# A decode layer on one core: the last 96 rows of w2 on 32 partitions, c and x in one transfer, the first load whole, and another order of TensorE's last work

## The chip, the core and the metric

The kernel runs on one core of a Trainium2 chip. The metric is the device time of one execution in microseconds; the median of several executions counts. A profiled execution lists the work of the engines (TensorE is PE, its weight loads PEld; VectorE is DVE, ScalarE is ACT, GpSimd is POOL, SyncE is SP), the DMA queues, and which event ended each wait.

## The reference

A layer with adaptive layer norm: attention of one new token over a cache, then a dense block with Mish. Two batches, D = 512, 32 heads of 128, 4096 cached keys a head, F = 1376, all float32.

```python
mod = (_silu(c) @ w_mod).reshape(c.shape[0], 6, 1, -1)
sa, ca, ga, sb, cb, gb = (mod[:, 0], mod[:, 1], mod[:, 2], mod[:, 3], mod[:, 4], mod[:, 5])
h = _layernorm(x, axis=-1) * (1 + ca) + sa
x = x + ga * _A_ref(h, A_k_cache, A_v_cache, A_wq, A_wo)
h = _layernorm(x, axis=-1) * (1 + cb) + sb
x = x + gb * _B_ref(h, B_w1, B_b1, B_w2)
```

`_A_ref` projects q with `wq`, takes softmax(q k / sqrt(128)) v for each head and projects with `wo`. `_B_ref` is `mish(h @ w1 + b1) @ w2`.

## The kernel before

**Loads.** All large inputs (297 MB, nearly all of it the caches) are laid out on the host as rows of 128 partitions and go through three rooms of 128 x 16384 floats (8 MB each, 64 KB a partition). `stream()` (L30) lists 36 loads. Load 0 is m01 (the two modulations of the first norm), wq 0 and wq 1 in one transfer of 4 MB, and k 0 in another of 4 MB. Loads 1 to 31 are one transfer of 8 MB each: the keys of a head, values that lie further back, now and then a piece of wq and wo. The last four hold the remaining values and weights in smaller transfers; load 35 has m3 and w1 in two, m5 and w2 in four (L62). `load(n)` (L133) issues a room's transfers on SP; `used(...)` (L145) issues load n + 3 when everything of load n has been used. So three rooms are asked for at the start, and the fourth when head 0's keys have been used. ACT issues three small transfers: c and x (L162, 8 rows each, on every 16th partition) and `bias` (L164, one row of 12 floats on each of 128 partitions).

**Start.** PE runs in program order: c's columns (`cps`), the two means of the first norm, then `fps`, a PSUM tile that starts with b1 for all hidden units (L269, from `bias`) and gets `h @ w1` much later; then modulation 0 (L271), the columns of the normed x, and q for eight heads (L294).

**Heads.** For each head VectorE multiplies the keys with q in place (`products`, L321) and sums over 128 (`sums`, L324); the end of the sums gives the room back. PE does the weighted sums of the values (`weighted_v`, L362) and the output projection, a few heads behind.

**Tail.** The last head, 31, is treated by itself. Its values come in two halves of `weighted_v` into bank `ov0`; between the halves stand four `fold` matmuls, which bring the output projection of the other heads into `xps` (L474), and modulation 4 (L478). After the halves come `value_sums`, `head_values` and `head_out_q` (L484), then the residual x2, the second norm (`centred`, `rstd`), modulation 3, `h2ps`, the product with w1 (L514), three matmuls that add it to `fps` (L529), modulation 5, the Mish on VectorE and ScalarE up to `actt` (L549), and the product with w2 into `yps` (L554). `busy(n)` (L297) issues matmuls whose result nobody reads.

The 1376 hidden units are 11 chunks of up to 128, each on partitions of its own; chunk 10 has 96 units, and its other 32 rows of w2 are zeros. `yps` takes the chunks in order, 4 matmuls of 128 columns a chunk, one for each group of 32 output partitions; an fp32 matmul is two instructions here. Then VectorE multiplies with modulation 5 and adds x2 (L562, L563), and SP writes the output. w2 lies in load 35 behind m5: chunks 0 to 4 come with m5, chunks 5 to 8 in a transfer of 1 MB, chunks 9 and 10 in 256 KB each.

Of the kernel before, what the change touches and what calls it, by code (L numbers as in the profile page):

```python
# [8 lines left out]
F32 = mybir.dt.float32  # L9
# [4 lines left out]
P = 128  # L14
# [8 lines left out]
    "k": BIG, "v": HALF, "wq": W, "wo": W, "m01": 2 * W, "m2": W, "m3": W, "m4": W, "m5": W,  # L23
    "w1": 4 * sum(WIDTHS), "w2": 512 * len(CHUNKS),
}
AHEAD = (14, 22)
ROW = 2 * BIG


def stream():  # L30


    order, n_v = [], 0
    for h in range(1, HEADS):
# [12 lines left out]
    loads = [[([("m01", 0), ("wq", 0), ("wq", 1)], (4 * W,)), ([("k", 0)], (BIG,))]]  # L47
    for _ in range(1, HEADS):
        row = []
        while size(row) < ROW:  # L50
            room = ROW - size(row)
            row += order.pop(next(i for i, x in enumerate(order) if size(x) <= room))
        loads.append([(row, (ROW,))])
    last = [("v", h, i) for h in range(HEADS - 4, HEADS) for i in range(2)]
    assert order == [[key] for key in last[:2]], order
    loads += [
        [(last[:2] + [("wo", 6), ("wo", 7), ("m2", 0)], (BIG + 3 * W,))],
        [(last[2:4], (BIG,)), (last[4:6], (BIG,))],
        [([("m4", 0)] + last[6:], (W + HALF, W, W))],
        [  # L60
            ([("m3", 0), ("w1", 0)], (W + 2 * sum(WIDTHS), 2 * sum(WIDTHS))),
            ([("m5", 0), ("w2", 0)], (W + 5 * 512, 4 * 512, 512, 512)),  # L62
        ],
    ]
    return loads
# [3 lines left out]
def kernel(  # L69
# [28 lines left out]
    SCALE = DH ** -0.5  # L98
    NCH = len(CHUNKS)

    const = ctx.enter_context(tc.tile_pool(name="const", bufs=1))
# [13 lines left out]
    def take(t, keys):  # L115
        lo = 0
        for key in keys:
            kind, n = key[:2]
            part = t[:, lo : lo + SIZES[kind]]
            lo += SIZES[kind]  # L120
            if kind == "k":
                k_t[n] = part.rearrange("p (j d) -> p j d", d=DH)
            elif kind == "v":
                v_t[n, key[2]] = part.rearrange("p (c n) -> p c n", n=512)
            elif kind in ("wq", "wo"):
                (wq_t if kind == "wq" else wo_t)[n] = part.rearrange("p (k n) -> p k n", k=G)
            else:
                w_t[kind] = part.rearrange("p (k n) -> p k n", k=NCH if kind == "w2" else G)

# [3 lines left out]
    def load(n):  # L133

        t = kvp.tile([P, ROW], F32, tag="room", name=f"room{n}", bufs=3)
        lo = 0
        for keys, srcs in loads[n]:
            take(t[:, lo:], keys)
            for src in srcs:
                nc.sync.dma_start(out=t[:, lo : lo + src.shape[-1]], in_=src)  # L140
                lo += src.shape[-1]
# [15 lines left out]

    cq = work.tile([P, P], F32, tag="xn", name="cq", bufs=1)
    xq = const.tile([P, P], F32, name="xq")
    for t, src in ((cq, head[0]), (xq, head[1])):  # L160
        nc.gpsimd.memset(t, 0.0)
        nc.scalar.dma_start(out=t[::TB, :], in_=src)  # L162
    bias = const.tile([P, NCH + 1], F32, name="bias")
    nc.scalar.dma_start(out=bias, in_=b1c)  # L164
# [28 lines left out]
    h2t = const.tile([P, G, R], F32, name="h2t")  # L193
    actt = const.tile([P, NCH, R], F32, name="actt")
    for t in (ct, h2t, actt):
# [71 lines left out]

    fps = psum.tile([P, 512], F32, tag="att2", name="fps", bufs=1)[:, : NJ * G * B]
    nc.tensor.matmul(fps, lhsT=ident, rhs=bias[:, :, None].to_broadcast([P, NJ * G, B]), start=True, stop=False, skip_group_check=True)  # L269

# [200 lines left out]
    xps = psum.tile([P, 512], F32, tag="att", name="xps", bufs=1)  # L471
    weighted_v(H - 1, 0, 1 - N % 2)
    for g in range(G):
# [54 lines left out]
    for j in range(NJ):  # L528
# [4 lines left out]
            start=False,  # L533
            stop=(j == NJ - 1),
            skip_group_check=True,
        )
    busy(6)
    gps = modulation("5", 1, wm5)
    f = const.tile([P, 3, NJ * G, B], F32, name="f")
    hid = fps.rearrange("p (n b) -> p n b", b=B)  # L540
# [7 lines left out]
    nc.vector.reciprocal(f[:, 2], f[:, 2])  # L548
    nc.vector.tensor_tensor(out=actt[:, :, ::TB], in0=f[:, 1, :NCH], in1=f[:, 2, :NCH], op=ALU.mult)  # L549

    yps = wide_ps("yps")
    for n in range(NCH):
        for t in range(G):
            nc.tensor.matmul(  # L554
                yps[R * t : R * (t + 1), :P],
                lhsT=actt[:, n, :],
                rhs=w2_t[:, n, P * t : P * (t + 1)],
                start=(n == 0),
                stop=(n == NCH - 1),
            )  # L560
# [6 lines left out]
def _lay_out(np, a):  # L567
# [19 lines left out]
    starts = np.cumsum((0,) + WIDTHS)  # L587
    b1c = np.zeros((P, 12), a["B_b1"].dtype)
    w2 = np.zeros((P, len(CHUNKS), 512), a["B_w2"].dtype)
    for n, (g, j) in enumerate(CHUNKS):  # L590
        f0 = starts[g] + P * j
        f1 = min(f0 + P, starts[g + 1])
        b1c[: f1 - f0, n] = a["B_b1"][f0:f1]
        w2[: f1 - f0, n] = a["B_w2"][f0:f1]

# [3 lines left out]
    def piece(kind, n, part=None):  # L599
# [3 lines left out]
    arrays = {  # L603
        "head": np.stack([q_rows(a["c"]), q_rows(a["A_x"])]),
        "b1c": b1c,
    }
    for n, parts in enumerate(stream()):
        for i, (keys, widths) in enumerate(parts):
            row = np.concatenate([piece(*key) for key in keys], axis=1)
            cuts = np.split(row, np.cumsum(widths)[:-1], axis=1)  # L610
            for j, t in enumerate(cuts):
                arrays[f"load{n}_{i}_{j}"] = np.ascontiguousarray(t)
    return arrays
# [24 lines left out]
```

## Time and profile before

| | |
|---|---|
| median of three runs | 698.67 us (698.63 to 698.77) |
| the profiled execution | 698.77 us |
| its span, first to last instruction | 696.9 us |
| mean granted clock of TensorE | 0.677 |
| DMA, mean over the span | 427 GB/s |
| VectorE, PE, ScalarE busy | 587.1, 284.6, 44.3 us |

A page gives busy time by engine, the span in 40 slices (each digit tenths of a slice), the DMA queues (packets, megabytes, share of 16 engines' time) and the chain of waits that ended last. In the chain in order of time each row is start, length and what the chain passed through. A timeline row has start, length, engine, line, operation, tiles written and read, shapes, count, and in brackets the idle time before it and what ended it. A row of stretches has the length and then, for each engine, busy time and count of instructions, at the end the granted clock, the share of DMA time and GB/s. A row of DMA issues has count, KB each and the time from issue to landing.

### The profile page before, as it was taken

To read this page: it belongs to the slowest core of one execution; us is meant where nothing else is said; L and a number is where in the kernel's file an instruction comes from. 1 tells how busy PE (TensorE), PEld (TensorE's weight loads), DVE (VectorE), ACT (ScalarE), POOL (GpSimd) and SP (SyncE) were. 2 spreads that over 40 slices of the span, in tenths; PEclk is the share of its full clock that TensorE was granted. 3 is DMA by queue.
4 is the path that set the end of the run, shared out by engine and by line. 5 is a ranking of instruction groups with operands and counts; after the bars stand their busy time and mean duration, and the time that the engine had idled before them with its cause. 6 is when DMAs were issued, how large, how long until landed. Compare 5 with 4: busy or idle time off the path is not lost.

```text
span 696.9 us, 3922 instructions
## 1 busy us (share of the span) xinstructions
PE 284.6 (41%) x1640; PEld 103.9 (15%) x1640; DVE 587.1 (84%) x219; ACT 44.3 (6%) x169; POOL 4.2 (1%) x20
## 2 busy tenths in 40 slices
PE   0603334335145615234342806234333425224697
PEld 0200011001011201101110301011101111001245
DVE  3399999999999999999999999999999999899002
ACT  1000000000000000000000000000000000000011
POOL 2000000000000000000000000000000000000000
PEclk9966656768565567656575656656575658556889
DMA  9999999999999999999999999999999999999996
GB/s 388 455 421 421 425 467 429 418 430 425 463 422 421 437 421 456 429 421 441 421 451 429 418 444 425 448 426 421 441 429 445 429 421 441 429 434 422 425 419 266
DMA packets 6690, 297.48 MB, mean 427 GB/s; under 512 B 888, under 2 KB 912, under 8 KB 1168
## 3 DMA queue, kind: packets, MB, share of 16 engines
q1 hardware_dynamic: 6496, 297.21, 98.9%
q8 instruction: 13, 0.21, 0.1%
q10 hardware_dynamic: 176, 0.01, 0.0%
q14 instruction: 5, 0.04, 0.0%
HBM read 297.22 MB, written 0.00 MB: 426 GB/s over the span
## 4 chain that ended last, share of the span: by engine, by line
DMA 63%; DVE 33%; PE 2%; issue 0%; SPq 0%; POOL 0%; ACT 0%; ACTq 0%; DVEq 0%; POOLq 0%
DMA room<-in_load 61%; DVE room L321 16%; DVE s L324 16%; DMA bias<-in_b1c 3%; PE ov L362 1%; PE qps L294 1%; PE modps L247 1%; PE yps L554 0%; SPq L140 0%; DVE m L337 0%; DVE hcw L283 0%; DVE m L329 0%; PE fps L269 0%; ACT q L295 0%; ACTq L162 0%
## 5 line engine op out<-in xcount | busy, mean ns | idle before, releaser
L321 DVE TENSOR_TENSOR room<-room,q 128x8192 f32<-128x8192 f32 x32 | 278.1, 8691 | 40.0 <-DMA room<-in_load 35.5
L324 DVE TENSOR_REDUCE s<-room 128x64 f32<-128x8192 f32 x32 | 277.9, 8683 | 0.0
L362 PE MATMUL ov<-room,e 128*32 128x512 f32 x1024 | 177.0, 841 | 73.5 <-ACT e L340 31.2
L333 PE MATMUL mt<-d,same 128*128 128x64 f32 x64 | 18.7, 388 | 194.0 <-DVE d L331 194.0
L362 PEld LDWEIGHTS ov<-room,e 128*32 128x32 f32 x1024 | 39.8, 146 | 180.8 <-issue 128.3
L340 ACT ACTIVATE e<-s,m 64x64 f32<-64x64 f32 x64 | 22.1, 345 | 547.9 <-DVE m L337 547.1
L333 PEld LDWEIGHTS mt<-d,same 128*128 128x128 f32 x64 | 13.5, 263 | 224.6 <-DVE d L331 177.6
L294 PE MATMUL qps<-room,hcw 128*128 128x512 f32 x64 | 40.7, 797 | 4.6 <-DMA room<-in_load 3.8
L348 PE MATMUL l<-l,ones 128*128 128x8 f32 x16 | 4.6, 359 | 73.7 <-ACT e L340 73.7
L385 PE MATMUL otp<-pick,o 128*128 128x8 f32 (+2 forms) x72 | 14.4, 328 | 37.3 <-ACT o L377 35.4
L377 DVE COPY o<-ov 128x256 f32<-128x256 f32 x1 | 0.4, 423 | 25.1 <-ACT o L377 25.1
L385 PEld LDWEIGHTS otp<-pick,o 128*128 128x128 f32 x72 | 13.6, 282 | 46.6 <-ACT o L377 43.7
L294 PEld LDWEIGHTS qps<-room,hcw 128*128 128x128 f32 x64 | 15.9, 261 | 24.4 <-issue 18.6
L348 PEld LDWEIGHTS l<-l,ones 128*128 128x128 f32 x16 | 3.8, 296 | 75.1 <-ACT e L340 75.1
L393 PE MATMUL att<-room,ot 128*32 128x512 f32 x62 | 10.9, 756 | 5.2 <-DMA room<-in_load 4.7
L337 DVE TENSOR_REDUCE m<-mt 128x1 f32<-128x64 f32 x32 | 6.9, 217 | 6.3 <-PE mt L333 6.3
L340 ACT ACTIVATION_READ_ACCUMULATOR e<-s,m 64x1 f32 x64 | 11.8, 185 | 0.0
L331 DVE TENSOR_SCALAR d<-half,m 128x64 f32<-128x64 f32 x32 | 8.1, 254 | 1.1
L273 DVE SCALAR_TENSOR_TENSOR hq<-modps,xn 128x128 f32<-128x128 f32 x1 | 0.3, 291 | 10.4 <-PE modps L247 10.4
L247 PE MATMUL modps<-room,ct 128*32 128x128 f32 (+1 forms) x160 | 8.1, 346 | 0.0
L329 DVE TENSOR_REDUCE m<-s 128x1 f32<-128x64 f32 x32 | 6.9, 217 | 0.9
L377 ACT COPY o<-ov 128x512 f32<-128x512 f32 (+1 forms) x9 | 5.1, 562 | 24.2 <-PE ov L362 24.1
(100 smaller groups left out, 68.5 us busy)
## 6 DMA issues: line engine op xcount, KB each, us to landing
room<-in_load SPq DMA_DIRECT2D x4, 4096.0 KB, 28.5
room<-in_load SPq DMA_DIRECT2D x1, 7168.0 KB, 39.1
room<-in_load SPq DMA_DIRECT2D x1, 3072.0 KB, 26.1
room<-in_load SPq DMA_DIRECT2D x3, 1024.0 KB, 22.3
room<-in_load SPq DMA_DIRECT2D x1, 2400.0 KB
room<-in_load SPq DMA_DIRECT2D x1, 2304.0 KB, 20.3
room<-in_load SPq DMA_DIRECT2D x1, 1376.0 KB, 15.2
room<-in_load SPq DMA_DIRECT2D x2, 256.0 KB, 22.6
```

Source lines behind the costliest of these rows:

```text
L247: nc.tensor.matmul(ps[R * g : R * (g + 1)], lhsT=ct[:, k, :], rhs=t[:, k, :].rearrange("p (m n) -> p m n", m=n)[:, :, P * g : P * (g + 1)] ...
L294: nc.tensor.matmul(ps, lhsT=hcw[:, k, :], rhs=wq_t[ch][:, k, :], start=(k == 0), stop=(k == G - 1))
L321: nc.vector.tensor_tensor(out=k_t[h], in0=k_t[h], in1=qv, op=ALU.mult)
L324: nc.vector.tensor_reduce(out=s_t[h], in_=k_t[h], axis=AX.X, op=ALU.add)
L329: nc.vector.tensor_reduce(out=m_t[h][:, 0:1], in_=s_t[h], axis=AX.X, op=ALU.max)
L331: nc.vector.tensor_scalar(out=d, in0=half, scalar1=m_t[h][:, 0:1], scalar2=None, op0=ALU.mult)
L333: nc.tensor.matmul(mps[h], lhsT=same, rhs=d, start=True, stop=True)
L340: nc.scalar.activation(e_t[i][own_b, :, M * i + 4 * b : M * i + 4 * b + 4], s_t[h][own_b].rearrange("p (c m) -> p c m", m=4), AF.Exp, bias ...
L348: nc.tensor.matmul(lps[n], lhsT=ones, rhs=sum_t[n % 2], start=True, stop=True)
L362: nc.tensor.matmul(ov[bank][R * g : R * (g + 1), :], lhsT=e_t[h % HC][:, NB // 2 * part + c, :], rhs=v_t[h, part][:, c, :], start=(first a ...
L385: nc.tensor.matmul(tps[:, x], lhsT=o_t[m], rhs=pick_t[n][:, m, x], start=(m == 0), stop=(m == 3),)
L393: nc.tensor.matmul(att[R * i : R * (i + 1), :], lhsT=ot_t[n % 2][:, i, :], rhs=wo_t[n][:, i, :], start=(n == 0), stop=(n == H // HC - (2 i ...
```

## The change

- w2's last 96 rows (chunk 10) lie on partitions 0 to 31, three rows a partition, instead of on 96 of 128 partitions with 32 of zeros. In the order of the load they come ahead of chunk 9, in four transfers of 8 rows of 6 KB (every fourth partition); chunk 9's 256 KB are the last transfer.
- Chunk 10 is thus three chunks of 32 rows: `actt`, `bias`, `fps` and `f` have 13 columns of chunks instead of 11 or 12, two more matmuls write units 32 to 63 and 64 to 95 of that chunk to partitions 0 to 31 of `fps`, and `yps` takes chunks 0 to 8, the three short ones with 32 contracted rows each, then chunk 9: 52 matmuls instead of 44.
- c and x lie side by side on the host and come in one transfer of 8 rows of 1 KB, with one memset instead of two.
- Load 0 is one transfer of 8 MB.
- PE's order in the tail: both halves of head 31's values and their sums first, then the fold matmuls, `busy(1)`, `head_values`, half of modulation 4, `head_out_q`, and the other half. Modulation 4 is no longer copied by `keep`; ScalarE adds 1 to it while it copies it to `m4`, and VectorE multiplies that with the centred x2. Two `busy` calls fall away and two are shorter.

```diff
-    "w1": 4 * sum(WIDTHS), "w2": 512 * len(CHUNKS),
+    "w1": 4 * sum(WIDTHS), "w2": 512 * (len(CHUNKS) + 2),
 }
+BAND = 32
+LOW = [3 * 512]
+N_FULL = len(CHUNKS) - 1
+ROWS = [(n, P) for n in range(N_FULL - 1)] + [(N_FULL + i, BAND) for i in range(3)] + [(N_FULL - 1, P)]
...
-    loads = [[([("m01", 0), ("wq", 0), ("wq", 1)], (4 * W,)), ([("k", 0)], (BIG,))]]
+    loads = [[([("m01", 0), ("wq", 0), ("wq", 1), ("k", 0)], (ROW,))]]
...
-            ([("m5", 0), ("w2", 0)], (W + 5 * 512, 4 * 512, 512, 512)),
+            ([("m5", 0), ("w2", 0)], (W + 5 * 512, 4 * 512, LOW, 512)),
...
             for src in srcs:
-                nc.sync.dma_start(out=t[:, lo : lo + src.shape[-1]], in_=src)
+                rows = [slice(i, BAND, 4) for i in range(4)] if src.shape[0] == BAND else [slice(0, P)]
+                for r in rows:
+                    nc.sync.dma_start(out=t[r, lo : lo + src.shape[-1]], in_=src[r])
                 lo += src.shape[-1]
...
-    cq = work.tile([P, P], F32, tag="xn", name="cq", bufs=1)
-    xq = const.tile([P, P], F32, name="xq")
-    for t, src in ((cq, head[0]), (xq, head[1])):
-        nc.gpsimd.memset(t, 0.0)
-        nc.scalar.dma_start(out=t[::TB, :], in_=src)
-    bias = const.tile([P, NCH + 1], F32, name="bias")
+    cx = const.tile([P, 2, P], F32, name="cx")
+    nc.gpsimd.memset(cx, 0.0)
+    nc.scalar.dma_start(out=cx[::TB], in_=head)
+    cq, xq = cx[:, 0, :], cx[:, 1, :]
+    bias = const.tile([P, NCH + 2], F32, name="bias")
...
-    weighted_v(H - 1, 0, 1 - N % 2)
+    for part in range(2):
+        weighted_v(H - 1, part, 1 - N % 2)
+    value_sums(1 - N % 2, (nc.scalar.copy, nc.vector.tensor_copy))
     for g in range(G):
         nc.tensor.matmul(
             xps[R * g : R * (g + 1), :P], lhsT=fold, rhs=att_sb[:, P * g : P * (g + 1)],
             start=True, stop=False, skip_group_check=True,
         )
-    keep(4, modulation("4", 1, w_t["m4"])[:, 0, :])
-    weighted_v(H - 1, 1, 1 - N % 2)
-    value_sums(1 - N % 2, (nc.scalar.copy, nc.vector.tensor_copy))
-    busy(2)
+    busy(1)
     head_values(N, HC - 1, HC)
-    busy(1)
+    mps4 = modulation("4", 1, w_t["m4"], ks=(0, 1))
     head_out_q(H - 1)
+    modulation("4", 1, w_t["m4"], mps4, (2, 3))
...
-    busy(2)
-    xc, var, rs = centred(x2, "b", add_x, lambda: busy(4))
+    nc.scalar.activation(m4, mps4[:, 0, :], AF.Copy, bias=1.0)
+    xc, var, rs = centred(x2, "b", add_x, lambda: busy(3))
...
-    nc.vector.scalar_tensor_tensor(m4, mod[4], 1.0, xc, op0=ALU.add, op1=ALU.mult)
+    nc.vector.tensor_tensor(out=m4, in0=xc, in1=m4, op=ALU.mult)
...
+    for i in (1, 2):
+        nc.tensor.matmul(
+            fps[:BAND, B * (N_FULL + i) : B * (N_FULL + i + 1)],
+            lhsT=hq_pad[:, P * J + BAND * i : P * J + BAND * (i + 1)], rhs=sel[:, GRP, :],
+            start=False, stop=(i == 2), skip_group_check=True,
+        )
...
-    for n in range(NCH):
+    for i, (n, k) in enumerate(ROWS):
         for t in range(G):
             nc.tensor.matmul(
                 yps[R * t : R * (t + 1), :P],
-                lhsT=actt[:, n, :],
-                rhs=w2_t[:, n, P * t : P * (t + 1)],
-                start=(n == 0),
-                stop=(n == NCH - 1),
+                lhsT=actt[:k, n, :],
+                rhs=w2_t[:k, i, P * t : P * (t + 1)],
+                start=(i == 0),
+                stop=(i == NCH + 1),
             )
```

The host's layout follows: `w2` and `b1c` by `ROWS`, `head` with c and x of a row side by side.

More of the change, by code (lines that the diff above doesn't have):

```diff
@@ L99 @@
     NCH = len(CHUNKS)
+    GRP, J = CHUNKS[-1]
     const = ctx.enter_context(tc.tile_pool(name="const", bufs=1))
@@ L127, in take @@
             else:
-                w_t[kind] = part.rearrange("p (k n) -> p k n", k=NCH if kind == "w2" else G)
+                w_t[kind] = part.rearrange("p (k n) -> p k n", k=NCH + 2 if kind == "w2" else G)
     w_t = {}
@@ L193 @@
     h2t = const.tile([P, G, R], F32, name="h2t")
-    actt = const.tile([P, NCH, R], F32, name="actt")
+    actt = const.tile([P, NCH + 2, R], F32, name="actt")
     for t in (ct, h2t, actt):
@@ L266 @@
     nc.vector.tensor_scalar(out=xn, in0=xc, scalar1=y0, scalar2=y1, op0=ALU.mult, op1=ALU.mult)
-    fps = psum.tile([P, 512], F32, tag="att2", name="fps", bufs=1)[:, : NJ * G * B]
-    nc.tensor.matmul(fps, lhsT=ident, rhs=bias[:, :, None].to_broadcast([P, NJ * G, B]), start=True, stop=False, skip_group_check=True)
+    fps = psum.tile([P, 512], F32, tag="att2", name="fps", bufs=1)[:, : (NCH + 2) * B]
+    nc.tensor.matmul(fps, lhsT=ident, rhs=bias[:, :, None].to_broadcast([P, NCH + 2, B]), start=True, stop=False, skip_group_check=True)
     ps = modulation("0", 2, w_t["m01"])
@@ L533 @@
             start=False,
-            stop=(j == NJ - 1),
+            stop=False,
             skip_group_check=True,
+        )
[4 more added lines that the diff above has]
+            start=False, stop=(i == 2), skip_group_check=True,
         )
@@ L538 @@
     gps = modulation("5", 1, wm5)
-    f = const.tile([P, 3, NJ * G, B], F32, name="f")
+    f = const.tile([P, 3, NCH + 2, B], F32, name="f")
     hid = fps.rearrange("p (n b) -> p n b", b=B)
@@ L548 @@
     nc.vector.reciprocal(f[:, 2], f[:, 2])
-    nc.vector.tensor_tensor(out=actt[:, :, ::TB], in0=f[:, 1, :NCH], in1=f[:, 2, :NCH], op=ALU.mult)
+    nc.vector.tensor_tensor(out=actt[:, :, ::TB], in0=f[:, 1], in1=f[:, 2], op=ALU.mult)
     yps = wide_ps("yps")
-    for n in range(NCH):
+    for i, (n, k) in enumerate(ROWS):
         for t in range(G):
@@ L587, in _lay_out @@
     starts = np.cumsum((0,) + WIDTHS)
[L588 to L594, printed above, removed]
+    b1c = np.zeros((P, len(ROWS)), a["B_b1"].dtype)
+    w2 = np.zeros((P, len(ROWS), 512), a["B_w2"].dtype)
+    for i, (n, k) in enumerate(ROWS):
+        g, j = CHUNKS[min(n, N_FULL)]
+        f0 = starts[g] + P * j + BAND * max(n - N_FULL, 0)
+        b1c[:k, n] = a["B_b1"][f0 : f0 + k]
+        w2[:k, i] = a["B_w2"][f0 : f0 + k]
     pieces = {**kv, "wq": wq, "wo": wo, "m01": [wm[:, :, :1024]], "w1": [w1], "w2": [w2]}
@@ L603, in _lay_out @@
     arrays = {
-        "head": np.stack([q_rows(a["c"]), q_rows(a["A_x"])]),
+        "head": np.stack([q_rows(a["c"]), q_rows(a["A_x"])], axis=1),
         "b1c": b1c,
@@ L609, in _lay_out @@
             row = np.concatenate([piece(*key) for key in keys], axis=1)
-            cuts = np.split(row, np.cumsum(widths)[:-1], axis=1)
-            for j, t in enumerate(cuts):
-                arrays[f"load{n}_{i}_{j}"] = np.ascontiguousarray(t)
+            lo = 0
+            for j, width in enumerate(widths):
+                width, k = (width[0], BAND) if isinstance(width, list) else (width, P)
+                arrays[f"load{n}_{i}_{j}"] = np.ascontiguousarray(row[:k, lo : lo + width])
+                lo += width
     return arrays
```

## The prediction

> **What bounds the kernel now.** I read the page first, its queues and its chain of waits, then the chain in order of time, then the timelines of the first 50 us and the last 10, with stretches and transfer landings where a wait had to be placed. The page:
>
> ```profile
> span 696.9 us, 3922 instructions
> ...
> PE 284.6 (41%) x1640; PEld 103.9 (15%) x1640; DVE 587.1 (84%) x219; ACT 44.3 (6%) x169; POOL 4.2 (1%) x20
> ...
> DMA  9999999999999999999999999999999999999996
> ...
> q1 hardware_dynamic: 6496, 297.21, 98.9%
> q8 instruction: 13, 0.21, 0.1%
> q10 hardware_dynamic: 176, 0.01, 0.0%
> ```
>
> The 16 DMA engines are full in every slice but the last. q1, the stream of loads issued by SP, has 98.9% of their time; no arithmetic engine comes near. So the time is: the start of the stream, its bytes, any moment at which it runs dry, and the tail behind its last landing. The change can act at three places: bytes (64 KB of 297 MB go, 0.15 us at the stream's rate), a dry moment, the tail. The profiled run took 698.77 us, of which 1.9 lie outside the span; the median of the three runs is 698.67. All sums below start from 698.77.
>
> The chain in order of time shows the start and when a room (load buffer) comes free:
>
> ```profile
> 2.79 17.57 DMA bias<-in_b1c
> 20.36 0.04 issue
> 20.40 0.62 PE fps L269 x2
> ...
> 30.87 8.70 DVE room L321
> ...
> 39.60 8.70 DVE s L324
> ...
> 48.32 0.23 DVE m L329
> ...
> 66.19 0.23 DVE m L329
> ...
> 102.08 38.23 DMA room<-in_load
> 140.31 0.02 issue
> 140.34 8.69 DVE room L321
> ...
> 198.42 8.69 DVE room L321
> ```
>
> PE stands at the bias matmul of L269 until the 6 KB of `bias` land at 20.36; behind it in PE's order stand modulation 0 and the q projection. From the release to the first product is 30.87 - 20.40 = 10.47 us, to the end of head 0's sums 48.32 - 20.40 = 27.9 us. There the fourth load is issued, since room 0 is free. The stream gives a room each (198.42 - 140.34) / 3 = 19.4 us, VectorE uses one each 66.19 - 48.32 = 17.9 us. VectorE starts late and catches up; its lateness costs nothing as long as the fourth load is queued before the third has ended.
>
> **First part: one whole first load, c and x together.** The small transfers on ACT's queue share the 16 engines with the stream:
>
> ```profile
> 0.74 0.39 SPq L140 DMA_DIRECT2D room<-in_load  x1
> ...
> 8.23 0.56 PE L237 MATMUL cps<-ident,cq 128*128 128x8 f32 x2 [8.23 <-DMA cq<-in_head]
> ...
> 10.57 0.29 DVE L206 TENSOR_REDUCE rs_a<-xq 128x1 f32<-128x128 f32 x1 [0.81 <-DMA xq<-in_head]
> ...
> 13.92 0.34 DVE L266 TENSOR_SCALAR xn<-xc_a,rs_a 128x128 f32<-128x128 f32 x1
> ```
> ```profile
> 1.50:2.00 0.50, 0.00 (x0) 0.00 (x0) 0.37 (x1) 0.00 (x0) 0.50 (x4) 1.00 2.21 590
> ...
> 15.00:20.00 5.00, 0.00 (x0) 0.00 (x0) 0.00 (x0) 0.00 (x0) 0.00 (x0) 1.00 1.01 433
> ```
>
> At 433 GB/s an engine moves 27 GB/s: a row of 32 KB (4 MB over 128 partitions) takes 1.21 us, one of 64 KB 2.42 us. q10 has 176 packets: 8 rows of c, 8 of x, 128 of bias, and 32 completion marks, which is one a transfer and engine if c and x use 8 engines each and bias 16. q1's 6496 come out in the same way (45 transfers of 128 rows and 16 marks, 16 packets for the output). So a partition's row is one packet, whatever its length. x lands 10.57 - 8.23 = 2.34 us behind c, which is 1.9 rows of 32 KB: a packet of data and a mark, one in each turn between two rows of the stream. bias lands 20.40 - 10.57 = 9.83 us behind x, 8.1 rows: eight packets and a mark, one of them beside the stream's own mark between the halves of the first load. The small transfers wait by turns, and a turn is as long as a row of the stream.
>
> The Trainium skill ("DMA: Bandwidth & Descriptors", Queues, rings and completion order) says that an engine drains a packet of some 9 to 17 descriptors from one queue before it changes to another. By it bias's eight descriptors would go in one turn and the sum would have no delay here; the 9.83 us say one descriptor a turn, and I go by them.
>
> After the change the rows beside them are 64 KB. c and x land together, without x's two turns; bias lands 8 turns of 2.42 us, 19.4 us, behind them. When c lands is less sure. Traffic starts in the stretch 1.50 to 2.00 (say 1.75); c is there at 8.23, 6.48 us later: four rows (4.84 us) and some 1.6 us of start and completion. With as many rows of double length c lands at 1.75 + 1.6 + 9.7 = 13.0 and bias at 32.4. If what goes ahead of it is fixed in bytes or in time, one long row fewer does: 10.6 and 30.0. The lowest, two rows fewer: 27.6. I take 30.0: that an engine has so many bytes under way seems a nearer reason for c's wait than a fixed number of rows, but no row of this trace decides it. The work on c and x (xn ends 3.7 us after x's landing) is done by 18, ahead of bias; the first load lands at about 1.75 + 19.4 + 0.5 = 21.7, so its being whole holds nothing up; the fewer SP and ACT issues save time on sequencers that wait anyway.
>
> Then the fourth load is issued at 30.0 + 27.9 = 57.9 instead of 48.3. When does the stream need it?
>
> ```profile
> 2.12 0.49 SPq L140 DMA_DIRECT2D room<-in_load  x1
> ```
> ```profile
> room<-in_load SPq DMA_DIRECT2D x1, 59.4
> ```
>
> The third load, issued at 2.12, lands at 61.5; its last bytes are through at about 61.0. From issue to traffic took 1.0 us at the start (0.74 to about 1.75), so an issue by 59.7 is in time. 57.9 leaves 1.8 us, each later room gains 19.4 - 17.9 = 1.5 us, and the first part costs nothing. What hides it is the 24 MB already queued; at a bias later than about 31.8 the cover is gone (rival B).
>
> **Second part: the tail.**
>
> ```profile
> 669.29 22.31 DMA room<-in_load
> 691.60 0.04 issue
> 691.65 1.30 PE yps L554 x40
> 692.95 0.02 issue
> 692.96 0.47 PE yps L554 x8
> ...
> 693.52 0.30 DVE y L562
> ...
> 693.85 0.29 DVE y L563
> ```
> ```profile
> 689.29 1.08 PE L247 MATMUL modps<-room,ct 128*32 128x128 f32 x32
> 689.40 0.20 DVE L549 TENSOR_TENSOR actt<-f 128x22 f32<-128x22 f32 x1
> ...
> 690.19 1.27 PE L554 MATMUL yps<-room,actt 128*32 128x128 f32 x40
> ```
> ```profile
> 690.50:691.00 0.50, 0.50 (x28) 0.50 (x24) 0.00 (x0) 0.21 (x1) 0.00 (x0) 1.00 0.44 168
> 691.00:691.50 0.50, 0.47 (x20) 0.20 (x8) 0.00 (x0) 0.00 (x0) 0.00 (x0) 1.00 0.32 123
> ```
>
> A chunk of yps is 8 instructions (two passes by four column groups). Chunks 0 to 4 run at 690.19; chunks 5 to 8 wait for the 1 MB transfer issued at 669.29 and start at 691.65; chunk 9 follows at once; chunk 10 starts at 692.96, when the last 256 KB have landed and PE is just free. Five chunks take 1.30 us, 0.26 each.
>
> *Removed:* one transfer of 256 KB, 16 KB an engine, 0.6 us. *Added:* four of 8 rows of 6 KB, 0.23 us a row: nothing on engines that they don't use, 0.9 us on those that they do. Which engines they get no row says. By the shares 0.44 and 0.32 more than half the engines are done by 691; on those the four are free, and the last landing comes 0.6 earlier, 692.3; on the late ones it comes 0.3 later, 693.2. SP's three more issues (0.43 us each) have nothing but the output behind them.
>
> *Added on PE:* the 96 rows are three chunks of 32 rows instead of one, in the order between chunk 8 and the last full one. The 1 MB transfer that releases chunk 5 has the same bytes ahead of it, so 691.65 stays. From there stand 4 + 3 + 1 = 8 chunks where 6 stood. No matmul of 32 contracted rows is in this trace; nearest is L554's own, with the same 128 columns streamed, so 0.26 a chunk: the last starts at 691.65 + 7 x 0.26 = 693.47, behind either landing, and +0.52 reaches the end. Below: if a short chunk were free, 6 - 1 = 5 chunks and the landing at 692.3 would start the last at about 692.7, -0.3; with the landing alone as bound, -0.6. Above: the last group takes 0.47 us where four matmuls fill 0.26, so emptying PE costs 0.21; twice (into and out of a shape of 32 rows) +0.4.
>
> That last bound has a rule behind it: the Trainium skill ("TensorEngine Tiling (Array Packing)", Tiling Modes) says that a change of tiling mode drains TensorE. By it the sum would have the 0.4. A change from 128*128 to 128*32 stands here without a visible gap:
>
> ```profile
> 681.16 0.35 PE L218 MATMUL var_b<-rs_b,mean_w 128*128 128x1 f32 x2
> 681.45 1.08 PE L247 MATMUL modps<-room,ct 128*32 128x128 f32 x32
> ```
>
> I leave it out.
>
> *Moved on PE:* the four fold matmuls and modulation 4 (1.08 us, as the row just shown) go behind the last head's second half, half of modulation 4 under ScalarE's copy. The path to x2 and so to `actt` becomes about a microsecond shorter; m4's addition goes to an idle ScalarE, two more matmuls into `fps` go in (four instructions, 0.13 us at the pace of yps). None of it counts: chunks 0 to 4 end at 690.19 + 1.27 = 691.46 already, and chunk 5 waits for its transfer until 691.65. Were that cover (0.19 us) gone, a later `actt` would reach the end in full; the order makes it earlier. The path comes nearer to the loads of m3, w1 and m5, whose waits at worst bring it back to where it was.
>
> **Sum:** start 0, bytes 0 (they no longer bind the last landing), tail +0.52: 698.77 + 0.52 = 699.3 us.
>
> **The rivals.**
> *B, the stream runs dry after the third load: slower.* Its place is the issue of load 3, its price begins when bias lands after 31.8. For it: turns counted in rows give 32.4. Issue at 60.3, traffic at 61.3 to 61.6, 0.3 to 0.6 dry, and a restart, for which c's 1.6 us beyond its four rows are the bound; I take half, 0.8. With it +1.3 over my sum: 700.6 us. Later rooms don't pay again, since VectorE gains 1.5 us on each. Against it: it needs a number of rows to be what is fixed.
> *C, the tail gains.* Short chunks cost far less than full ones, and the earlier landing counts: 698.77 - 0.6 = 698.2 us. For it: they load a quarter of the weights. Against it: they stream as many columns.
> *D, nothing of the small transfers slows down and the drain is paid:* 698.77 + 0.9 = 699.7.
>
> **How the numbers follow.** My forecast 0.48, D 0.07, B 0.33 with what is larger than it (a stall twice as long, 702), C 0.12. The likeliest's own range is 698.9 to 699.8. To hold 8 in 10 the range takes C's end and B: 698.2 to 701.2. No change is told apart below 0.2%, 1.4 us, here: slower means above 700.1, which is B and a little of the upper end of D, 0.37; faster needs 697.3, below C's price: 0.05; the rest 0.58.
>
> **What would show it.** First part: `bias` released at L269 near 30 (27.6 to 32.4) instead of 20.4, and one turn apart from c by 19.4; the first product 10.5 later; the fourth load issued near 58; DMA share 0.97 or more between 58 and 65. A dip there, and a third-to-fourth landing gap over 20 us, is B. Bias near 20 would overturn the turns. Second part: chunk 5 released at the same distance from the stream's end, eight chunks of 0.26 without a wait for the last transfer; a wait there, or short chunks well under 0.26, is C; a gap at the change of shape is D. My reasons fall if the span shortens, or if the stream itself, from first to last landing, changes by more than 0.5 us without a dry moment.

## The result, and the profile after

| | before | after |
|---|---|---|
| median | 698.77 us (698.63 to 699.48) | 700.41 us (699.09 to 701.69) |
| profiled execution | 698.77 us | 700.66 us |
| its span | 696.9 us | 698.8 us |

18 runs of each stand behind the medians. The ratio is 1.0022, with an interval of 95% from 1.0015 to 1.0029: slower by 0.22%, just over what can be told from no change. 700.41 lies inside the range that was forecast, but the forecast itself, 699.3, is met by the quickest runs only; the median stands where rival B was put (700.6). By the prediction's own line (slower means above 700.1, chance 0.37) the change made the kernel slower. The runs of the new kernel also lie 2.6 us apart, those of the old one 0.85. Three executions of the experiments below took 737 to 739 us (one of b_w2, two of a_quarter), a slower state of the chip, and are left out of all medians and ratios.

The page of the kernel after, its queues:

```profile
q1 hardware_dynamic: 6272, 297.15, 98.7%
...
q10 hardware_dynamic: 160, 0.01, 0.0%
```

The packets bear out how they were counted. Small transfers: 8 + 8 marks for c and x together, 128 + 16 for bias, 160. The stream has 224 fewer: 128 rows and 16 marks for the two halves that became one, and 144 for the transfer of chunk 10, against 4 x (8 + 8) = 64 now. So a transfer of 8 rows runs on 8 engines.

The chain of waits in order of time (start, length, what it passed through), from the start to head 0's sums:

```profile
2.26 27.58 DMA bias<-in_b1c
...
29.88 0.63 PE fps L275 x2
30.51 3.61 PE modps L253 x32
...
36.20 5.21 PE qps L300 x8
...
42.05 8.70 DVE room L327
50.78 8.70 DVE s L330
59.50 0.23 DVE m L335
```

and the timeline of SP's DMA queue behind it:

```profile
59.55 0.33 SPq L147 DMA_DIRECT2D room<-in_load  x1
```

bias lands at 29.9 where 30.0 was forecast. But from its release to the first product it takes 42.05 - 29.88 = 12.17 us instead of 10.47: the first eight instructions of the q projection alone need 5.21 us, and 3.71 in the kernel before. The fourth load is issued at 59.55, not at 57.9.

What that does to the stream shows in any later room. The landing of the same load, in the chain of the kernel before and of the kernel after:

```profile
332.12 40.52 DMA room<-in_load
```
```profile
333.69 40.49 DMA room<-in_load
```

It is at 374.18 instead of 372.64, 1.54 us late, long before the tail; in all experiments below but b_whole it lies between 372.31 and 372.92. The half-microseconds at the passage from the third load to the fourth show where this arises. First one row of the kernel before, then five of the kernel after (the last two columns are the share of DMA time and GB/s):

```profile
60.50:61.00 0.50, 0.50 (x8) 0.06 (x4) 0.50 (x1) 0.00 (x0) 0.00 (x0) 0.50 4.26 1835
```
```profile
60.50:61.00 0.50, 0.25 (x2) 0.06 (x1) 0.50 (x1) 0.00 (x0) 0.00 (x0) 0.50 4.50 1573
61.00:61.50 0.50, 0.00 (x0) 0.00 (x0) 0.50 (x1) 0.00 (x0) 0.00 (x0) 0.50 0.39 131
61.50:62.00 0.50, 0.00 (x0) 0.00 (x0) 0.50 (x1) 0.00 (x0) 0.00 (x0) 0.50 0.37 131
62.00:62.50 0.50, 0.00 (x0) 0.00 (x0) 0.50 (x1) 0.00 (x0) 0.00 (x0) 0.50 0.43 131
62.50:63.00 0.50, 0.00 (x0) 0.00 (x0) 0.50 (x1) 0.00 (x0) 0.00 (x0) 0.50 0.41 131
```

A packet is booked where it starts, and 131 GB/s over half a microsecond are one row of 64 KB. In the kernel before, 14 of the 16 engines start a row in this half-microsecond (1835 / 131) and the other two in the ones beside it; a row takes 4.26 x 0.5 x 16 / 14 = 2.43 us. In the kernel after, 12 engines start in it (1573 / 131), 1.0 to 1.4 us behind the issue, and the other four one by one, the last some 3 us behind the issue; the 12 rows take 4.50 x 0.5 x 16 / 12 = 3.00 us each. So the engines take up the fourth load partly late and all slowly. The share of DMA time doesn't show it, since a slow row counts as busy: over 58 to 65 us it is 1.09, and 1.04 in the kernel before. The dip that the prediction named as a sign of rival B isn't there, though B is what happened.

The end of the chain after, and the weight loads of the same time from the timeline:

```profile
669.90 23.05 DMA room<-in_load
...
693.00 2.27 PE yps L566 x64
...
695.36 0.30 DVE y L574
```
```profile
693.00 0.81 PEld L566 LDWEIGHTS yps<-room,actt 128*32 128x32 f32 x32 [0.49 <-DMA room<-in_load]
694.01 0.59 PEld L566 LDWEIGHTS yps<-room,actt 32*32 32x32 f32 x24 [0.20 <-issue]
694.80 0.16 PEld L566 LDWEIGHTS yps<-room,actt 128*32 128x32 f32 x8 [0.20 <-issue]
```

Chunk 5 is released 1.35 us later than before (693.00, 691.65); that is the stream's delay. Its size isn't the same all along, since other landings of both kernels vary too: the chains have 1.54 us at 374, 2.48 at 491 (488.82 before) and 0.90 at 663 (662.24 before). From there to the last two instructions of VectorE it takes 695.36 - 693.00 = 2.36 us, before 693.52 - 691.65 = 1.87: 0.49 more. 64 instructions run without a wait, 32 full, 24 short, 8 full. At each change of shape the weight loads pause for 0.20 us (the brackets), but the matmuls don't: at the pace of the kernel before (1.30 us for 40, and 0.21 to empty PE) 64 would take 2.29 us, and they take 2.27. 1.35 + 0.49 = 1.84 is the whole of the 1.89 us between the two profiled runs.

### The profile page after: what moved, and what is told of

It reads as the page before. It is cut to its first block, busy times and chain, and to the rows that moved or that the text cites. A ratio compares the mean times of both kernels' runs of the same rounds, so it can differ in the third digit from the quotient of the medians.

```text
span 698.8 us, 3954 instructions
## 1 busy us (share of the span) xinstructions
PE 278.2 (40%) x1656; PEld 102.2 (15%) x1656; DVE 584.7 (84%) x219; ACT 44.3 (6%) x169; POOL 4.3 (1%) x19
## 4 chain that ended last, share of the span: by engine, by line
DVE 48%; DMA 48%; PE 3%; issue 0%; SPq 0%; POOL 0%; ACT 0%; DVEq 0%; POOLq 0%
DMA room<-in_load 44%; DVE s L330 24%; DVE room L327 24%; DMA bias<-in_b1c 4%; PE ov L368 1%; PE qps L300 1%; PE modps L253 1%; DVE d L337 0%; DVE m L335 0%; PE yps L566 0%; SPq L147 0%; DVE m L343 0%; DVE hcw L289 0%; PE fps L275 0%; PE hps L243 0%
## 5 line engine op out<-in xcount | busy, mean ns | idle before, releaser
L327 DVE TENSOR_TENSOR room<-room,q 128x8192 f32<-128x8192 f32 x32 | 278.1, 8690 | 31.8 <-DMA room<-in_load 25.8
L368 PE MATMUL ov<-room,e 128*32 128x512 f32 x1024 | 173.0, 826 | 70.2 <-ACT e L346 30.2
```

Source lines behind the costliest of these rows:

```text
L327: nc.vector.tensor_tensor(out=k_t[h], in0=k_t[h], in1=qv, op=ALU.mult)
L368: nc.tensor.matmul(ov[bank][R * g : R * (g + 1), :], lhsT=e_t[h % HC][:, NB // 2 * part + c, :], rhs=v_t[h, part][:, c, :], start=(first a ...
```

## The experiments

The theory: the whole first load delays bias, bias delays the fourth load, and the stream runs dry for a varying time. The rival: the tail and the layout of w2 make the excess. In the jobs that follow the kernel before stands at 698.92, 698.89 and 698.83 us. A ratio is that to the kernel before, with its interval.

**Parts undone and parts alone.** a_split is the kernel after with the first load in two halves:

```diff
-    loads = [[([("m01", 0), ("wq", 0), ("wq", 1), ("k", 0)], (ROW,))]]
+    loads = [[([("m01", 0), ("wq", 0), ("wq", 1)], (4 * W,)), ([("k", 0)], (BIG,))]]
```

> The changed kernel with the first load in two transfers of 4 MB again, all else as changed. Turns theory (a small transfer waits one row of the stream a turn, and a row is 32 KB again): c and x land near 8.2 and bias 9.8 later, near 18, earlier than the 20.4 of before; the fourth load is issued near 46, the stream has no dry moment, and the only loss left is the tail's two more chunks, +0.5: 699.2 us, with a spread of its runs as narrow as that of the kernel before (under 1 us). Rival (the loss lies in the tail or in w2's 8-row transfers): the time stays at 700.4 with runs between 699 and 702.

b_whole is the kernel before with the opposite edit alone; c and x stay apart.

```diff
-    loads = [[([("m01", 0), ("wq", 0), ("wq", 1)], (4 * W,)), ([("k", 0)], (BIG,))]]
+    loads = [[([("m01", 0), ("wq", 0), ("wq", 1), ("k", 0)], (ROW,))]]
```

> The kernel before with one edit, the first load whole; c and x stay two transfers. Turns theory: c lands near 10.6, x two turns of 2.42 us behind it at 15.4, bias 19.4 behind x near 34.9; with 27.9 us from there (29.6 if TensorE runs slow after its idle time) the fourth load is issued at 62.8 to 64.5, the engines stand dry from 61 to 64 or 66, and the time is 3 to 5 us over the kernel before: 702 to 704 us. Rival (the wait is for the whole first load to land, at 22): the first product starts near 33, nothing runs dry, 698.8 us.

b_w2 is the kernel before with the edits of w2's rows alone, b_pe with PE's order and modulation 4's addition alone. Of their diffs, the line of each that says most:

```diff
-            ([("m5", 0), ("w2", 0)], (W + 5 * 512, 4 * 512, 512, 512)),
+            ([("m5", 0), ("w2", 0)], (W + 5 * 512, 4 * 512, LOW, 512)),
```
```diff
-    weighted_v(H - 1, 0, 1 - N % 2)
+    for part in range(2):
+        weighted_v(H - 1, part, 1 - N % 2)
...
-    keep(4, modulation("4", 1, w_t["m4"])[:, 0, :])
-    weighted_v(H - 1, 1, 1 - N % 2)
```

> The kernel before with w2's last 96 rows as in the change (three chunks of 32 rows, four transfers of 8 rows, chunk 9 last); start and order of the tail as before. Theory of the prediction: eight chunks stand behind chunk 5's release where six stood, +0.5, 699.2 to 699.3 us. Rival (short chunks are nearly free and the earlier last landing counts): 698.2 to 698.8 us.

> The kernel before with the changed order of the tail on TensorE alone (values of head 31 together, modulation 4 split, its copy with the added 1). Theory: actt is ready about a microsecond earlier, and the wait for chunk 5's transfer takes all of it: 698.7 us, within 0.2 of before. Rival (the path of arithmetic from the last values to actt sets the end): 697.7 us.

| | median us | ratio | interval |
|---|---|---|---|
| a_split | 698.92 | 1.0001 | 0.9992 to 1.0009 |
| b_whole | 702.90 | 1.0066 | 1.0054 to 1.0078 |
| b_w2 | 699.57 | 1.0007 | 0.9998 to 1.0016 |
| b_pe | 698.76 | 0.9997 | 0.9988 to 1.0006 |

The first load alone, undone, takes the whole excess away; alone, it costs more than the change does as a whole. So the tail and w2's layout aren't the reason of the excess. The chain of a_split:

```profile
2.26 15.33 DMA bias<-in_b1c
...
17.63 0.63 PE fps L275 x2
...
31.08 8.70 DVE room L327
...
331.79 40.65 DMA room<-in_load
...
691.08 2.27 PE yps L566 x64
...
693.44 0.30 DVE y L574
```

The room lands at 372.44 again. The tail has the same 2.36 us from release to y as in the kernel after; but chunk 5 is released at 691.08, 0.57 ahead of the kernel before, which hides the longer work. The chain of b_whole, its SP queue and its stretches:

```profile
2.77 31.94 DMA bias<-in_b1c
...
34.76 0.62 PE fps L269 x2
...
45.23 8.70 DVE room L321
...
336.39 40.51 DMA room<-in_load
```
```profile
62.72 0.33 SPq L140 DMA_DIRECT2D room<-in_load  x1
```
```profile
61.00:62.00 1.00, 0.00 (x0) 0.00 (x0) 1.00 (x1) 0.00 (x0) 0.00 (x0) 0.50 0.00 0
62.00:63.00 1.00, 0.00 (x0) 0.00 (x0) 0.93 (x3) 0.00 (x0) 0.00 (x0) 0.50 0.00 0
```

With c and x apart bias waits two turns more and lands at 34.8. The fourth load is issued at 62.72, no packet starts between 61 and 63, and the room lands at 376.90, 4.26 late. 702.90 - 698.92 = 3.98 us reach the end. Its six runs lie between 702.72 and 705.86 us; the profiled one (702.80), with 10.47 us from the release to the first product (45.23 - 34.76), is among the quickest. Here all engines stand still at once, and the dry moment can be seen directly; in the kernel after only a part of them starts late.

The two kernels give the last moment at which the fourth load could have been issued: 62.72 - 4.26 = 58.5 in b_whole, and 59.55 - 1.74 = 57.8 in the kernel after against a_split's landing. Each is good to some 0.5 us, since that landing varies by 0.6 us in the kernels without a delay.

b_w2's median is 0.65 us higher, with an interval that reaches 1. In its profile PE is the bound at the end, not the transfer; two rows of its chain:

```profile
661.89 6.23 PE ov L369 x32
...
691.14 3.15 PE yps L567 x104
```

All 13 chunks run in one go, so `actt` came when w2 had landed. A possible reason is in the first row: the weighted sum of the values behind the 661.9 landing took 6.23 us where it took 5.38 in the kernel before. But b_pe took 6.19 there and lost nothing, so the reason stays open. b_pe is level, as was said of the order. a_split has both edits and stands at 698.92, as if the order won back what w2 adds; but the intervals of the three overlap, so this is a reading and not shown.

**The wait for bias taken off the path, and PE kept busy.** a_fps is the kernel after with the bias matmul behind the first q projections, so that nothing ahead of head 0 waits for bias:

```diff
-    nc.tensor.matmul(fps, lhsT=ident, rhs=bias[:, :, None].to_broadcast([P, NCH + 2, B]), start=True, stop=False, skip_group_check=True)
...
     project_q(1)
+    nc.tensor.matmul(fps, lhsT=ident, rhs=bias[:, :, None].to_broadcast([P, NCH + 2, B]), start=True, stop=False, skip_group_check=True)
```

a_warm is the kernel after with 13 matmuls of 512 columns, whose result nobody reads, ahead of the bias matmul:

```diff
+    for _ in range(13):
+        nc.tensor.matmul(ov[1], lhsT=ident, rhs=ident[:, None, :].to_broadcast([P, 4, P]), start=True, stop=True)
```

> The changed kernel with the bias matmul of fps moved on TensorE behind the q projection, so that nothing in front of the first product waits for bias; bias itself still lands late. Theory (late bias, then TensorE slow after idling, then a dry stream): modulation 0 starts when the first load has landed, near 22.8; even with a slow TensorE (12.2 us to the first product, as in the profile of the changed kernel) head 0's sums end near 52.5, the stream never runs dry, and the time is that of the split first load, 698.9 us, with runs within 0.6 us. Rival (8 MB in one transfer cost time by themselves): 700.4 stays.

> The changed kernel with 13 more matmuls of 512 columns in front of fps (their result is read by nobody), which keep TensorE busy from 14.3 until bias lands. Theory (the spread of the changed kernel's runs is TensorE at half speed for a varying time after its 15.6 us of idling): bias still at 29.9, but hps and qps run at full speed, the first product 10.5 us after the release, near 40.4, the fourth load issued near 57.8, no dry moment: 698.9 to 699.2 us and runs within 0.7 us. Rival (late bias alone makes the dry moment, TensorE's speed has no part): 700.4 us, runs between 699 and 702 as before.

a_fps: 698.79 us, ratio 0.9999 (0.9990 to 1.0008), all runs between 698.66 and 699.41. a_warm: 699.12 us, ratio 1.0004 (0.9995 to 1.0012), 698.82 to 699.94. Both take away the loss and most of the spread, and both leave the whole first load and the tail as they are. The chain of a_fps:

```profile
22.70 3.67 PE modps L253 x32
...
32.60 8.70 DVE room L326
```

Modulation 0 waits for the first load itself now, and the first product is 9.45 us earlier. In a_warm bias lands as late as in the kernel after, and only PE's speed differs. PE's timeline in a_warm (start, length, engine, line, tiles, shapes, count, idle time before), then the row of the kernel after that answers to its last:

```profile
14.11 13.77 PE L276 MATMUL ov<-ident 128*128 128x512 f32 x26
29.85 0.40 PE L277 MATMUL fps<-bias,ident 128*128 128x26 f32 x2 [1.97 <-DMA bias<-in_b1c]
30.18 1.93 PE L253 MATMUL modps<-room,ct 128*32 128x256 f32 x32
```
```profile
29.88 0.63 PE L275 MATMUL fps<-bias,ident 128*128 128x26 f32 x2 [15.61 <-DMA bias<-in_b1c]
30.44 3.64 PE L253 MATMUL modps<-room,ct 128*32 128x256 f32 x32
```

The same 32 instructions take 1.93 us where PE was kept busy and 3.64 behind 15.61 us of idling. The first product comes 8.54 us after the release (38.39 - 29.85), the fourth load is issued at 55.88, and the room lands at 331.83 + 40.48 = 372.31: no delay. So the kernel after loses its time because bias is late *and* because PE comes back slowly.

**The turns at a third length.** a_quarter is the kernel after with the first load in four transfers of 2 MB, rows of 16 KB:

```diff
-    loads = [[([("m01", 0), ("wq", 0), ("wq", 1), ("k", 0)], (ROW,))]]
+    loads = [[([("m01", 0), ("wq", 0), ("wq", 1), ("k", 0)], (2 * W, 2 * W, HALF, HALF))]]
```

> The changed kernel with the first load in four transfers of 2 MB, so that a row is 16 KB and a turn 0.61 us. Turns theory: bias 8 to 9 turns behind c and x, 5 us (9.7 with 32 KB, 19.3 with 64 KB), landing near 11 to 12 us, and modulation 0 waits for its own quarter, near 7 to 12; the fourth load is issued before 42. The stream was not dry with 4 MB either, so the time is 698.9 us again. Rival (bias's delay is a fixed time and not a row of the stream a turn): bias stays near 17.

```profile
7.40 0.57 PE L243 MATMUL cps<-ident,cx 128*128 128x8 f32 x2 [7.40 <-DMA cx<-in_head]
...
12.28 0.63 PE L275 MATMUL fps<-bias,ident 128*128 128x26 f32 x2 [1.15 <-DMA bias<-in_b1c]
```

PE's timeline shows bias 4.88 us behind c. With rows of 32 KB (a_split, c at 7.93) it is 9.70, with 64 KB (after, c at 10.54) 19.34. Doubling the row doubles the distance: eight rows' turns each time, with rows of 0.61, 1.21 and 2.42 us. The time was 699.33 us, ratio 1.0007 (0.9998 to 1.0017): nothing is gained by a bias that is earlier than needed.

**Attempts at a faster kernel.** In the tail some engines end earlier than others. b_bal is the kernel before with the second 4 MB of load 33 cut into transfers of 112, 8 and 8 rows, so that half of the engines get more rows than the others; b_bal2 does it with seven transfers of 16 spread rows and two of 8:

```diff
+                rows = [slice(0, 112), slice(112, 120), slice(120, P)] if n == 33 and lo else [slice(0, P)]
```
```diff
+                rows = [slice(i, P, 8) for i in range(7)] + [slice(7, P, 16), slice(15, P, 16)] if n == 33 and lo else [slice(0, P)]
```

> The kernel before with one edit in load 33: its second 4 MB transfer (values of heads 30 and 31's predecessor, 32 KB a partition) in one of 112 rows and two of 8 rows. Theory (DMA's falling shares behind 689 are engines that lag by 1.4 us for each 16 KB instruction fetch that they served, and transfers of 8 rows go to the eight engines that serve none): the lagging engines carry 7 rows instead of 8 and are 1.2 us earlier, with all landings behind it; time 697.5 to 697.9 us. Rival (8-row transfers go to engines that lag as much as the others): 698.9 or up to 1.2 us more.

> The kernel before with load 33's second 4 MB transfer in seven transfers of 16 rows (every eighth partition) and two of 8 rows (every sixteenth), so that no two engines write neighbouring partitions at a time. Theory of the lag (the engines that serve instruction fetches are late, 8-row transfers go to the other eight): the late engines carry one row of 32 KB less, 1.2 us, and every landing behind it comes earlier: 697.6 to 698.2 us, the less the more TensorE's own order binds the tail. Rival (8-row transfers go to engines that lag too): 698.9 or up to 1.2 us more.

They took 714.29 us (ratio 1.0217, 1.0203 to 1.0231) and 713.84 (1.0212, 1.0198 to 1.0226): a clear miss. The stretch 650 to 655 us in the kernel before, b_bal and b_bal2:

```profile
650.00:655.00 5.00, 2.95 (x18) 0.91 (x20) 0.64 (x3) 0.97 (x5) 0.00 (x0) 0.78 1.02 431
```
```profile
650.00:655.00 5.00, 1.20 (x20) 0.77 (x16) 0.64 (x3) 1.14 (x5) 0.00 (x0) 0.91 0.97 220
```
```profile
650.00:655.00 5.00, 1.25 (x24) 0.82 (x13) 0.64 (x3) 1.14 (x5) 0.00 (x0) 0.93 1.00 200
```

The engines are as busy as before and move half as much. b_bal's 8-row transfers were on neighbouring partitions, b_bal2's are spread, and both are slow, so neighbourhood isn't the reason; it stays open. Whether the engines that served instruction fetches carry the lag, as the theory had it, these runs can't say. b_bal2 with PE's new order (b_bal2_pe) and with the tail of a_split (s_bal2) took 714.23 us (1.0220, 1.0206 to 1.0234) and 714.77 (1.0226, 1.0213 to 1.0240), which says nothing on the tails.

> As the run before, with the changed order of the tail on TensorE. Theory: with the loads earlier, TensorE's order sets the end of b_bal2 in part, so this one is 0.2 to 0.6 us faster than it: 697.3 to 697.8 us. Rival (order without part, as on its own): the same time as b_bal2.

> All of the change but the whole first load, with load 33's second transfer split as in b_bal2. Theory: the late engines gain the same 1.2 us, but eight chunks still stand behind chunk 5's release, so 0.2 to 0.5 us slower than b_bal2_pe: 697.7 to 698.2 us. Rival (w2's short chunks free): as fast as b_bal2_pe or faster.

s_adj is a_split with w2's four transfers on neighbouring partitions (0 to 7, 8 to 15 and so on) instead of every fourth:

```diff
-                rows = [slice(i, BAND, 4) for i in range(4)] if src.shape[0] == BAND else [slice(0, P)]
+                rows = [slice(8 * i, 8 * i + 8) for i in range(4)] if src.shape[0] == BAND else [slice(0, P)]
```

> The changed kernel with the split first load and one more edit: the four 8-row transfers of w2's last rows write 8 neighbouring partitions each instead of every fourth. Theory from the run with 8-row transfers to neighbouring partitions (its 32 KB rows took 2.3 to 4.2 us instead of 1.2): the eight engines then share one way into those partitions, so a transfer of 8 x 6 KB takes about 1.9 us instead of 0.24, four of them some 7 us instead of 1; the last chunk's transfer behind them ends 4 to 6 us later: 703 to 705 us. Rival (the 15 us came from the transfer of 112 rows): 698.9 us, as with every fourth partition.

```profile
691.92 2.27 PE yps L566 x64
```

699.79 us, ratio 1.0013 (1.0004 to 1.0022). Chunk 5 is released 0.84 later than in a_split, and the time is 0.87 longer. The direction was expected; the size is a fraction of it, and it is hardly clear of the variation between kernels with transfers to every fourth partition: a_fps and a_quarter release chunk 5 at 691.61 and 691.74, and their times are 698.79 and 699.33. No version beat both kernels: b_pe and a_fps are level with the kernel before.

## Why the prediction was right or wrong

**Turns: right.** bias at 29.9 (forecast 30.0), c at 10.54 (10.6), 19.34 apart (19.4). Of the three answers for c the middle one was right, and a_quarter gives the same turn at a third row length. The reason given for c isn't shown, so that this part came out right in part by luck: c lands at 7.40, 7.93 and 10.54 us for rows of 16, 32 and 64 KB, which by the forecast's own terms (start at 1.75, 1.6 us beyond the rows) is 6.6, 3.8 and 3.0 rows, or about 106, 121 and 190 KB. Neither rows nor bytes alone are fixed. The Trainium skill's rule on arbitration ("DMA: Bandwidth & Descriptors", Queues, rings and completion order), by which bias's eight descriptors would go in one turn, doesn't hold between these two queues: three row lengths show one row a turn.

**"The first part costs nothing": wrong.** The step that failed is the 27.9 us from bias's release to the end of head 0's sums, carried over unchanged from the kernel before. It measured 59.50 - 29.88 = 29.62. The difference is PE's speed: the instructions of the q projection between 30 and 46 us (shortest, median, longest in ns), and a stretch of the same time, in the kernel after:

```profile
L300 PE MATMUL qps<-room,hcw x16: 592/592/1222, 36.2 to 44.2; 128*128 128x512 f32 x16
```
```profile
36.00:40.00 4.00, 3.80 (x6) 1.77 (x7) 0.14 (x1) 0.00 (x0) 0.00 (x0) 1.00 1.21 524
```

The granted clock of the stretch is 1.00 while matmuls take up to 1222 ns instead of 592; the column doesn't show this state, the length of an instruction does. It isn't the length of the idling either that decides. PE's rows of the bias matmul in the kernel before, in b_whole and in b_pe, with the idle time ahead of it in brackets, and the first product in b_pe's chain:

```profile
20.40 0.62 PE L269 MATMUL fps<-bias,ident 128*128 128x24 f32 x2 [7.54 <-DMA bias<-in_b1c]
```
```profile
34.76 0.62 PE L269 MATMUL fps<-bias,ident 128*128 128x24 f32 x2 [17.13 <-DMA bias<-in_b1c]
```
```profile
20.23 0.62 PE L269 MATMUL fps<-bias,ident 128*128 128x24 f32 x2 [7.52 <-DMA bias<-in_b1c]
```
```profile
33.80 8.70 DVE room L321
```

All come back slow (0.62 us for what takes 0.40 in a_warm). After 7.54 and 17.13 us of idling the first product came 10.47 us behind the release, after the 15.61 of the kernel after 12.17, in a_split 13.45 (31.08 - 17.63). b_pe has the same start as the kernel before and idles as long, and took 13.57 (33.80 - 20.23); with that start b_bal2_pe took 10.48 and b_bal 12.10. So 10.47 was one draw of something that lies between 10.47 and 13.57 where PE has idled, and the quickest one.

The Trainium skill ("TensorE: Matmul & The Clock Gate", Part 1: The HAM clock gate) says that the array's clock is halved once PE has idled for about 3.4 us and restored after a window of that length in which it was busy, and that the windows run free, so that the number of slow matmuls differs from run to run. The 1222 and 592 ns and the distances just named agree with it. An estimate from its 3.4 us: the bias matmul and modulation 0 keep PE busy for some 4.2 us without a gap, which holds a whole window for some positions of it and not for others, and behind them stand two gaps.

**The cover was also shorter than taken.** The forecast said an issue by 59.7 is in time; the runs put that at 57.8 to 58.5. At 57.9 the forecast stood on the edge without its 1.8 us of reserve. The two errors, 1.65 in the issue and 1.2 to 1.9 in the cover, use up the reserve and make the stream's delay. In what the cover fell short the half-microseconds above show: the forecast took 1.0 us from issue to traffic for all engines and then rows at full pace; 12 engines took 1.0 to 1.4 us, the last of the other four some 3, and the first rows lasted 3.00 us instead of 2.43. Why a load that is issued this late is taken up so stays open.

**The spread follows.** With bias at 29.88 and 17.45 us from the first product to the end of the sums, 10.47 to 13.57 us in between put the issue at 57.8 to 60.9 us, which against a limit of 57.8 is a loss of 0 to 3.1 us; the runs span 2.6. Only one of them has a trace, so this is worked out and not shown; that the runs of a_warm and a_fps, where PE is kept busy or doesn't wait for bias, span 1.1 and 0.75 us supports it, and so do the 3.1 us of b_whole.

**Rival B** was the right mechanism with the right place. Its condition was wrong: bias later than 31.8 isn't needed, 29.9 is enough. That 700.6 is near the median of 700.41 is partly luck: it was worked out for another lateness of bias, with PE's 10.47 us unchanged. That the range holds the result is owed to B too: it was stretched to 701.2 for B, while the range of the likeliest case ended at 699.8. B got no more than 0.33 because one profile's 10.47 us was taken as fixed and the cover as 1.2 to 1.9 us longer than it was.

**The tail: right in PE's work.** +0.49 us from release to y (forecast +0.52). The short chunks run at the pace of full ones, so C falls; PE's matmuls have no gap at the change of shape to 32*32 and back, so D falls as well. That it reaches the end in full was too simple. In a_split, a_fps and a_quarter, which have the new tail and no delay of the stream, chunk 5's release varies between 691.08 and 691.74, and their times, 698.79 to 699.33, lie between 0.1 us below the kernel before of their job and 0.4 above it. "The 1 MB transfer that releases chunk 5 has the same bytes ahead of it, so 691.65 stays" is true to half a microsecond, which is as much as the term itself.

**PE's order and the bytes: as forecast**, nothing that can be measured; b_pe is 0.16 us below the kernel before, inside its interval. The bytes were not tried by themselves.

## What to carry to other kernels

Here a small transfer on another queue than the large stream waited one row of the stream for each row that an engine had to move for it (eight for bias: 4.88, 9.70 and 19.34 us beside rows of 16, 32 and 64 KB), so making the stream's first transfers larger delays everything small behind them in proportion; look which instruction waits for the small one in program order, and move that instruction back where its result isn't needed yet. Where TensorE has idled ahead of a chain, one profile's duration of that chain is one draw (10.47 to 13.57 us here); a cover of less than 3 us on it was none. When a delay is suspected in a stream, compare the landings of the same load in both kernels, and count the rows that start in short stretches where the shift begins; the share of DMA time may not show it.

## What the runs showed that wasn't expected

With w2 in its new layout the stream ran a little faster: from the landing near 198 us to the one near 606 the chains of a_split, a_fps, a_quarter, s_adj, s_bal2 and b_w2 take 407.68 to 407.92 us, those of the kernel before, b_pe, b_bal, b_bal2 and b_bal2_pe 407.94 to 408.10, some 0.2 us more. It may be part of why the longer tail didn't show in a_split. The cause was not sought.

Cutting one transfer of 4 MB late in the stream into pieces of 112 + 8 + 8 rows, or into pieces of 16 and 8, halved the rate to 200 to 220 GB/s with the engines as busy as before, and cost 15 us (b_bal, b_bal2). Four transfers of 8 rows at the very end cost 0.87 us more on neighbouring partitions than on every fourth (s_adj against a_split), and some 0.5 us more than in a_quarter, which has them on every fourth too.
